# First values loaded plainly and summed on VectorE, second keys and values pooled by TensorE, in a kernel whose order a planner writes

## The chip, the cores and the metric

The kernel runs on one core of a Trainium2 chip. The metric is the device time of one execution in microseconds (us); the median of three runs stands for a kernel. The engines named below are TensorE (PE, its weight loads PEld), VectorE (DVE), ScalarE (ACT), GpSimd (POOL) and SP, which only issues transfers. All transfers share 16 DMA engines.

## The reference, cut to what matters

Three layers follow one another, for 8 sequences of 576 tokens with 8 heads of 64 channels (4608 tokens, 512 channels). Only the first two matter here.

```python
k_p = k.reshape(B, H, 72, 8, D).mean(axis=3)      # pooled keys: 8 tokens to one
v_p = v.reshape(B, H, 72, 8, D).mean(axis=3)      # pooled values
attn = softmax(q @ k_p.T / sqrt(D))               # 576 x 72 for each head
x = attn @ v_p                                    # -> (4608, 512)
h = x @ w_in; g = h * sigmoid(h); y = g @ w_out   # 512 -> 2048 -> 512
```

A third layer routes every token to one of 8 experts or past them.

## The kernel before, in words

**Attention.** The 4608 queries are 36 tiles of 128 tokens. For tile `i` the kernel loads `q` (SP), makes the scores of all heads (`sc_all`, TensorE), the maxima (`mx_all`, VectorE), the exponentials (`ex_half`, ScalarE), their normalisation (`ns_all`, `nr_half`), a transpose (`pt_half`), its copy (`pc_half`), and the product with the pooled values (`pv_all`). `x_copy` (operation `xc`) puts the result into `xs`. A tile needs the pooled keys `kT` and pooled values of the sequences `b` its tokens lie in: tiles 0 to 3 of sequence 0 alone, tile 4 of sequences 0 and 1.

**Pooling.** The first keys (`k_load`, four transfers of 288 KB) arrive plainly and VectorE sums them with a strided reduction (`k_pool`, L325). Everything else is pooled by the DMA engines. For each sequence there are two accumulators for keys (`kA`) and two for values (`vp_at(b)`, `vB`). The first of four slices is loaded plainly by SP, and the other three are added on arrival (`pool_in`, L320, `accum_op=ALU.add`, issued by GpSimd). Each of these 144 KB transfers waits until the one before it on the same accumulator has landed. Then one addition of the two halves follows (`k_half` into `kT`, L333; `v_pool`, L349).

**The dense layer.** Its weights come as 16 transfers of 512 KB (`load_w`, L221, three buffers `stages`). Each is turned into float by two passes of ScalarE (`conv_low` L245, `conv_abs` L241) and two of VectorE (`conv_mix` L249, `conv_or` L254), then split into a high part (ScalarE, L281) and a low part (VectorE, L285). Activations are split likewise (`x_hi` L450, `x_lo` L454). The tokens go in 9 groups of 512; the first two groups use the plain product `whole` (L488, operations `pl`), the later ones a scheme with fewer products (L468). The activated results go through `outs` to memory.

**What sets the order.** `dense()` lists every operation with its possible engines, a cost in us on each, and the operations it waits for. `schedule()` keeps a clock for each engine, for the DMA queue and for buffers, and always takes the ready operation of greatest height: its longest chain of costs to the end, plus a bonus from the table `BONUS` by kind and phase. The order written in this way is fixed; on the chip each engine runs its own list in order, and waits at its head. So SP's transfers, too, wait behind one another. The planner decides on which of two engines some operations run.

```python
op(("k", b, r), {u: cost}, lambda e, b=b, r=r: k_add(b, r), [("k", b, r - 1)] if r % 4 else last_k, ...)
height[n] = min(ops[n][0].values()) + ops[n][4] + max((SIGNAL + height[u] for u in users[n]), default=0)
```

## Time and profile before

| what | us |
|---|---|
| median of 3 runs | 1274.11 |
| lowest and highest | 1271.37, 1277.19 |
| the profiled execution | 1271.41 |
| its span, first to last instruction | 1269.7 |
| TensorE busy in the span | 1219.1 (96%) |
| VectorE busy | 911.3 (72%) |
| ScalarE busy | 635.5 (50%) |
| GpSimd busy | 292.2 (23%) |

TensorE's busy time is an average: the first slices of the span have 30% and 70%, nearly all others 90% or more. The plain DMA queue takes 41.3% of the 16 engines' time for 172.26 MB, the adding and indirect queue 10.7% for 27.72 MB. In the rows further down, L12 is line 12 of the kernel, an arrow in brackets names what ended an engine's idle time, and a tile's buffers have no numbers. TensorE works a float32 product off in two rows, so a product of tile 0's scores (4 calls) shows as x8.

### The profile page before, as it was taken

The numbers are of one execution on the slowest core, as the hardware profiler recorded it, in microseconds if no ns is written. First come the engines' busy times: TensorE is split into PE (matmuls) and PEld (weight loads), VectorE is DVE, ScalarE is ACT, GpSimd is POOL, SyncE is SP. The second block draws the span as 40 slices with busy tenths as digits, with TensorE's granted clock in tenths as the row PEclk, the third lists the DMA queues.
The fourth block names the chain that finished last, engine by engine and source line by source line (L and its number), as shares of the span: only waits on it lengthen the run. The fifth ranks groups of instructions, "written<-read, shape, count | busy, mean of one in ns | idle before, by whom it ended". The sixth has DMA issues, their size and how long they took to land.

```text
span 1269.7 us, 24001 instructions
## 1 busy us (share of the span) xinstructions
PE 1219.1 (96%) x8148; PEld 1092.4 (86%) x8148; DVE 911.3 (72%) x2428; ACT 635.5 (50%) x1802; POOL 292.2 (23%) x289
## 2 busy tenths in 40 slices
PE   3799999999999999999999999999999999999997
PEld 3599989999999999978878888888888888888886
DVE  5786887776777778858988889888973445544572
ACT  5866677778777777722222222323331434443441
POOL 4232122112100000013423324242621212112121
PEclk9899999999999999999999999999999999999999
DMA  8896455646543337764434454454623444455642
GB/s 236 219 224 162 122 125 159 160 149 176 149 144 128 111 126 247 240 252 163 124 127 151 133 163 135 139 159 121 214 100 110 125 164 154 140 168 175 242 154 69
DMA packets 99414, 201.79 MB, mean 159 GB/s; under 512 B 17159, under 2 KB 35591, under 8 KB 99136
## 3 DMA queue, kind: packets, MB, share of 16 engines
q1 hardware_dynamic: 82736, 172.26, 41.3%
q0 software_dynamic: 16528, 27.72, 10.7%
q8 instruction: 71, 1.16, 0.4%
q14 instruction: 79, 0.65, 0.2%
HBM read 173.89 MB, written 66.99 MB: 190 GB/s over the span
## 4 chain that ended last, share of the span: by engine, by line
PE 56%; issue 20%; DMA 9%; DVE 8%; ACT 4%; POOLq 2%; POOL 1%; SPq 0%; another core or an unknown queue 0%; ACTq 0%; DVEq 0%
PE bk L468 17%; PE bk L571 10%; PE bk L572 9%; PE bk L573 9%; PE bk L488 3%; DMA stages<-in_w_in_dram 2%; PE bk L418 2%; PE bk L407 2%; PE bk L377 2%; POOLq L1489 2%; DMA room<-in_v_dram 2%; ACT room L391 1%; DVE room L591 1%; DMA room<-vd 1%; DMA out_dram<-xs,room 1%
## 5 line engine op out<-in xcount | busy, mean ns | idle before, releaser
L468 PE MATMUL bk<-ra,w7h 128*128 128x256 f32 x1088 | 200.6, 284 | 2.1 <-ACT outs L510 1.8
L556 ACT CAST w7h<-outs 128x512 fp32r<-128x512 f32 x142 | 87.8, 622 | 216.2 <-PE bk L572 183.9
L591 DVE SCALAR_TENSOR_TENSOR room<-bk,room 128x512 bf16<-128x512 f32 x272 | 187.9, 691 | 9.0
L571 PE MATMUL bk<-w7h 128*128 128x512 f32 x468 | 184.4, 394 | 1.5 <-ACT w7h L299 1.5
L572 PE MATMUL bk<-w7l,w7h 128*128 128x512 f32 x468 | 182.9, 391 | 0.2 <-DVE w7l L303 0.2
L573 PE MATMUL bk<-w7h,w7l 128*128 128x512 f32 x468 | 182.6, 390 | 0.0
L468 PEld LDWEIGHTS bk<-ra,w7h 128*128 128x128 f32 x1088 | 166.9, 189 | 4.1 <-ACT outs L510 2.8
L468 PE MATMUL bk<-ra,w7l 128*128 128x256 f32 x544 | 152.4, 280 | 0.0
L560 POOL TENSOR_TENSOR w7l<-outs,w7h 128x512 fp32r<-128x512 f32 x70 | 91.0, 1318 | 106.2 <-DVE room L591 80.3
L571 PEld LDWEIGHTS bk<-w7h 128*128 128x128 f32 x468 | 88.2, 188 | 19.7 <-ACT w7h L299 1.9
L1418 PE MATMUL p<-w7h 128*128 128x256 f32 x352 | 100.3, 285 | 4.8 <-PEq L1666 1.7
L573 PEld LDWEIGHTS bk<-w7h,w7l 128*128 128x128 f32 x468 | 88.3, 189 | 18.4
L572 PEld LDWEIGHTS bk<-w7l,w7h 128*128 128x128 f32 x468 | 88.3, 189 | 18.3 <-DVE w7l L303 0.5
L468 PEld LDWEIGHTS bk<-ra,w7l 128*128 128x128 f32 x544 | 102.8, 189 | 0.0
L1421 ACT ACTIVATE w7h<-p 128x256 fp32r<-128x256 f32 x88 | 33.5, 385 | 136.4 <-PE p L1420 123.4
L1419 PE MATMUL p<-w7l,w7h 128*128 128x256 f32 x352 | 99.8, 283 | 0.4 <-DVE w7l L1404 0.2
L1420 PE MATMUL p<-w7h,w7l 128*128 128x256 f32 x352 | 99.6, 283 | 0.0
L1422 DVE SCALAR_TENSOR_TENSOR w7l<-p,w7h 128x256 fp32r<-128x256 f32 x88 | 36.8, 424 | 83.7 <-ACT w7h L1421 60.6
L514 DVE TENSOR_TENSOR outs<-outs,bk 128x256 f32<-128x256 f32 x168 | 69.9, 417 | 35.4 <-PE bk L468 14.0
L488 PE MATMUL bk<-ra,w7h 128*128 128x256 f32 x512 | 93.6, 285 | 1.2 <-DVE ra L454 0.6
L391 ACT ACTIVATE room<-bk,mx 128x72 f32<-128x72 f32 x288 | 89.1, 334 | 9.6 <-PE bk L468 5.6
L468 PE MATMUL bk<-rb,w7h 128*128 128x256 f32 x480 | 91.1, 285 | 2.8 <-ACT outs L510 2.6
(268 smaller groups left out, 2982.1 us busy)
## 6 DMA issues: line engine op xcount, KB each, us to landing
outs<-gd SPq DMA_DIRECT2D x71, 512.0 KB
gd<-outs SPq DMA_DIRECT2D x56, 512.0 KB
outs<-in_w_dram SPq DMA_DIRECT2D x56, 512.0 KB
late<-in_w_dram SPq DMA_DIRECT2D x48, 512.0 KB
room<-in_w_dram SPq DMA_DIRECT2D x44, 512.0 KB
room<-in_q_dram SPq DMA_DIRECT2D x36, 256.0 KB
out_dram<-xs SPq DMA_DIRECT2D x36, 256.0 KB
x2d<-xs SPq DMA_DIRECT2D x36, 256.0 KB
```

Of the source, the lines that this page charges most:

```text
L391: nc.scalar.activation(out=P_t[i][:, h], in_=heads(ps)[:, h % HP], func=ACTF.Exp, scale=esc, bias=mx_t[i][:, h], accum_out=sm_t[i][:, h])
L468: nc.tensor.matmul(out=ps, lhsT=a[:, kk], rhs=b[:, kk], start=first, stop=end, skip_group_check=on)
L488: nc.tensor.matmul(out=ps, lhsT=a[:, kk], rhs=b[:, kk], start=first, stop=end)
L556: nc.scalar.copy(out=hi, in_=src)
L560: eng.tensor_tensor(out=lo, in0=src, in1=hi.bitcast(F32), op=ALU.subtract)
L571: nc.tensor.matmul(out=ps, lhsT=gh[:, ts], rhs=vh, start=first, stop=False)
L572: nc.tensor.matmul(out=ps, lhsT=gh[:, ts], rhs=vl, start=False, stop=False)
L573: nc.tensor.matmul(out=ps, lhsT=gl[:, ts], rhs=vh, start=False, stop=end)
L591: nc.vector.scalar_tensor_tensor(out=junk, in0=x, scalar=scale, in1=wb[:, e * DM:e * DM + DM], op0=ALU.mult, op1=ALU.mult, accum_out=lg_t[ ...
L1418: nc.tensor.matmul(out=ps, lhsT=W1h4[:, kk, m], rhs=xh[:, kk], start=(kk == 0), stop=False)
L1419: nc.tensor.matmul(out=ps, lhsT=W1h4[:, kk, m], rhs=xl[:, kk], start=False, stop=False)
L1420: nc.tensor.matmul(out=ps, lhsT=W1l4[:, kk, m], rhs=xh[:, kk], start=False, stop=(kk == KD - 1))
```

## The change

The first keys stay as they are, but their copy into `kT` becomes an operation of its own (`kc`). The first values get a layout of their own (`v0`, 72 partitions of 8 x 512) and come in two plain transfers (`v_load`, operations `vr 0`, six slices and two slices). VectorE reduces the six in two halves (`v_part`) and adds the other two (`v_rest`, the last is `vc 0`).

The second keys and values come unpooled, tokens on partitions (`kr`, `vr`: each 512 tokens in one transfer and 64 in another). A band matrix of ones, made by GpSimd at the start in the buffer `part`, sums 8 tokens at a time on TensorE: `k_sum` (`kp`, 20 calls of 72 columns) and `v_sum` (`vq`, 5 calls of 512 columns). Copies put the sums where the adding transfers put them before. Sequences 2 to 7 are pooled as before.

The raw tokens lie in buffers that are used later for something else. Hence new waits: the second keys lie in `outs` and `xs`, so the first plain product and `xc` of tile 2 wait for `kp`, the tail of the second keys and `xc` of tile 0 for `vc 0`; the second values lie in a part that later holds the operands of the second group, which wait for `vq`.

The planner charges adding transfers to the queue of all transfers (`ADDS`), which it did not before. Most costs of transfers are smaller (a 512 KB weight load 1.58 instead of 1.95), some others differ slightly, the bonuses have more phases, and all of their values differ.

```diff
@@ -45,34 +45,48 @@
-    "k": {0: 7196.1, 1: -24839.1, 2: -18055.7}, "kput": {0: 9234.7}, "v": {0: 36837.6, 1: -6003.6, 2: -5925},
...
+    "k": {0: 1087.5, 2: -20638.4, 3: -23245.3}, "kput": {0: 11444.8}, "kc": {0: 1225.9, 1: -61.5},
+    "vr": {0: 2969.2, 1: -4389.3}, "vn": {0: -2354.1}, "vc": {0: -5540, 1: 704.2}, "kr": {1: 2437.1},
...
@@ -183,8 +200,15 @@
+        band = part[:, 0:64 + SP]
+            nc.gpsimd.memset(band, 1.0)
+            nc.gpsimd.affine_select(out=band, in_=band, pattern=[[-POOL, 64 + SP]], base=64 * POOL + 1, channel_multiplier=1,
+                                    compare_op=ALU.is_gt, fill=0.0)
+            nc.gpsimd.affine_select(out=band, in_=band, pattern=[[POOL, 64 + SP]], base=POOL - 64 * POOL, channel_multiplier=-1,
+                                    compare_op=ALU.is_gt, fill=0.0)
...
@@ -315,27 +339,71 @@
...
+        def v_load(n):
+            t = (xs[0:SP, 1024:2048] if n else raws[0:SP]).rearrange("p (r c) -> p r c", c=DM)
+            nc.sync.dma_start(out=t, in_=v0[:, 6 * n:6 + 2 * n])
+        def v_part(n):
+            c = slice(n * 256, n * 256 + 256)
+            nc.vector.tensor_reduce(out=vp_at(0)[:, c], in_=raws[0:SP].rearrange("p (r c) -> p c r", c=DM)[:, c], axis=AX.X,
+                                    op=ALU.add)
+        def v_rest(n):
+            a, b, x = xs[0:SP, 1024:1536], xs[0:SP, 1536:2048], vp_at(0)
+            nc.vector.tensor_tensor(out=x if n else a, in0=a, in1=x if n else b, op=ALU.add)
+        raw_t = {"k": (outs[0], xs[:, 1536:2048]), "v": (raws[:, 0:2048], raws[:, 2048:2560])}
+        def raw_load(c, n):
+            src, t = kr if c == "k" else vr, raw_t[c][n]
+            if n:
+                nc.sync.dma_start(out=t[0:64], in_=src[512:576])
+            else:
+                nc.sync.dma_start(out=t.rearrange("p (j c) -> p j c", c=512), in_=src[0:512].rearrange("(j p) c -> p j c", p=128))
+        def raw_at(c, j):
+            t = raw_t[c]
+            return t[0][:, j * 512:j * 512 + 512] if j < 4 else t[1][0:64]
+        def band_at(j):
+            return band[0:128 if j < 4 else 64, 64 - 16 * j:64 - 16 * j + SP]
+        def k_sum(ps):
+            for hp in range(HP):
+                for j in range(5):
+                    nc.tensor.matmul(out=heads(ps)[:, hp], lhsT=raw_at("k", j)[:, hp * 128:hp * 128 + 128],
+                                     rhs=band_at(j), start=j == 0, stop=j == 4)
+        def v_sum(ps):
+            for j in range(5):
+                nc.tensor.matmul(out=ps[0:SP], lhsT=band_at(j), rhs=raw_at("v", j), start=j == 0, stop=j == 4)
+        def k_put(eng, h, ps):
+            p = slice(64 * h, 64 * h + 64)
+            copy(eng, kT[1][p, :, h], heads(ps)[p])
...
@@ -767,40 +841,55 @@
             for hp in range(HP):
-                op(("k", 0, hp), {"S": 1.1}, lambda e, hp=hp: put_in(("k", 0, hp), k_load(hp)))
-                op(("kput", 0, hp), {"V": 0.7}, lambda e, hp=hp: k_pool(hp, st["k", 0, hp]), [("k", 0, hp)])
-            for b in range((tiles * 128 - 1) // S + 1):
-                old = b > 1 and ((b - 1) * S - 1) // 128
-                last_k = [("kh", b - 1, h) for h in range(2)] if b else []
+                op(("k", 0, hp), {"S": 0.89}, lambda e, hp=hp: put_in(("k", 0, hp), k_load(hp)))
+                op(("kput", 0, hp), {"V": 1.13}, lambda e, hp=hp: k_pool(hp, st["k", 0, hp]), [("k", 0, hp)])
+            for h in range(2):
+                op(("kc", 0, h), {"A": 0.33, "V": 0.37}, lambda e, h=h: k_first(e, h), [("kput", 0, hp) for hp in range(HP)])
+            for n in range(2):
+                op(("vr", 0, n), {"S": (2.7, 0.95)[n]}, lambda e, n=n: v_load(n))
+                op(("vn", 0, n), {"V": 1.65}, lambda e, n=n: v_part(n), [("vr", 0, 0)])
+            op(("vn", 0, 2), {"V": 0.6}, lambda e: v_rest(0), [("vr", 0, 1)])
+            op(("vc", 0), {"V": 0.6}, lambda e: v_rest(1), [("vn", 0, n) for n in range(3)])
+            for n, cost in ((0, 3.1), (1, 0.4)):
+                for c in "kv":
+                    op((c + "r", 1, n), {"S": cost}, lambda e, c=c, n=n: raw_load(c, n), [("kput", 0, hp) for hp in range(HP)] if c == "k" else [("vn", 0, 0), ("vn", 0, 1)])
+            ops["kr", 1, 1][2].append(("vc", 0))
+            op(("kp", 1), {"T": 2.7}, lambda e: k_sum(bk["kp", 1]), [("kr", 1, 0), ("kr", 1, 1)], [B(("kp", 1))])
+            op(("vq", 1), {"T": 4.3}, lambda e: v_sum(bk["vq", 1]), [("vr", 1, 0), ("vr", 1, 1)], [B(("vq", 1))])
+            last["kp", 1], last["vq", 1] = keyed(1), [vdone(1)]
+            for h in range(2):
+                op(("kc", 1, h), {"A": 0.3, "V": 0.37}, lambda e, h=h: k_put(e, h, bk["kp", 1]), [("kp", 1)])
+            op(("vc", 1), {"A": 0.48, "V": 0.6}, lambda e: copy(e, vp_at(1), bk["vq", 1][0:SP]), [("vq", 1)])
+            for b in range(2, (tiles * 128 - 1) // S + 1):
+                old = ((b - 1) * S - 1) // 128
+                last_k = keyed(b - 1) + (b == 2) * [("xc", 3)]
                 for r in range(POOL):
-                    u, cost, lag = ("G", 1.1, 3.3) if r % 4 else ("S", 0.55, 0.0)
-                    if b:
-                        op(("k", b, r), {u: cost}, lambda e, b=b, r=r: k_add(b, r), [("k", b, r - 1)] if r % 4 else last_k, linger=(b == 1) * 1.5 + lag if lag else lag)
+                    u, cost, lag = ("G", 1.1, 1.3) if r % 4 else ("S", 0.44, 0.0)
+                    op(("k", b, r), {u: cost}, lambda e, b=b, r=r: k_add(b, r), [("k", b, r - 1)] if r % 4 else last_k, linger=lag)
                     op(("v", b, r), {u: cost}, lambda e, b=b, r=r: v_add(b, r),
-                       [("v", b, r - 1) if r % 4 else b > 0 and ("vput", b - 1), r == 0 and b > 1 and pe("pv", old)], linger=(b == 1) * 1.5 + lag if lag else lag)
+                       [("v", b, r - 1) if r % 4 else vdone(b - 1), r == 0 and pe("pv", old), b == 2 and r == 4 and ("xc", 3)], linger=lag)
                 for h in range(2):
-                    free, cost = [b > 1 and pe("sc", old)], {"V": 0.37, "G": 0.7}
-                    if b == 0:
-                        free, cost = [], {"A": 0.3, "V": 0.37}
-                    done = [("k", b, 3), ("k", b, 7)] if b else [("kput", 0, hp) for hp in range(HP)]
-                    op(("kh", b, h), cost, lambda e, b=b, h=h: k_half(b, h, e), done + free)
+                    op(("kh", b, h), {"V": 0.37, "G": 0.7}, lambda e, b=b, h=h: k_half(b, h, e), [("k", b, 3), ("k", b, 7), pe("sc", old)])
                 op(("vput", b), {"V": 0.6, "G": 1.23}, lambda e, b=b: v_pool(vp_at(b), vp_at(b), vB, e), [("v", b, 3), ("v", b, 7)])
...
-                   [pe("pv", i)] + (s > 0) * [(c, s - 1, k) for c in ("xh", "xl") for k in ((((0, 1), (7, 2)) if s <= PLAIN else ((3, 6), (5, 4)))[th])]
+                   [pe("pv", i), i == 2 and ("kp", 1), i == 0 and ("vc", 0)] + (s > 0) * [(c, s - 1, k) for c in ("xh", "xl") for k in ((((0, 1), (7, 2)) if s <= PLAIN else ((3, 6), (5, 4)))[th])]
+                    if 3 < slot < 7 and not free:
+                        free = [[("vq", 1)]]
-                        deps = [prev, *[("xl", s, k) for k in ((0, 1), (7, 2))[c // 2]], s == 0 and ("wl", p, c % 2)]
+                        deps = [prev or ("kp", 1), *[("xl", s, k) for k in ((0, 1), (7, 2))[c // 2]], s == 0 and ("wl", p, c % 2)]
...
@@ -995,13 +1086,14 @@
-            SHARED = ("ns", "mix", "or", "um", "uo", "wl", "ws", "vl", "xl", "xd", "sv", "nr", "vsum", "vput", "gl", "dot", "kput", "kh", "wc", "ra", "rg",
+            SHARED = ("ns", "mix", "or", "um", "uo", "wl", "ws", "vl", "xl", "xd", "sv", "nr", "vsum", "vput", "vn", "vc0", "gl", "dot", "kput", "kh", "wc", "ra", "rg",
+            ADDS, LAG, PULL = ("k", "v"), 1.0, 0.94
@@ -1076,6 +1168,8 @@
+                        if n[0] in ADDS:
+                            return t, t, max(queue[0], t + c + LAG) + PULL, u
@@ -1097,6 +1191,8 @@
+                if u == "G" and n[0] in ADDS:
+                    queue[0], free[u] = t1, t + ops[n][0][u]
```

## Rows read from the trace of the kernel before

**Rows 1.** Stretches: length, busy us of PE, PEld, DVE, ACT, POOL, PEclk, DMA, GB/s

```profile
0.00:41.40 41.40, 19.42 (x105) 15.14 (x105) 21.91 (x45) 24.45 (x80) 18.00 (x32) 1.00 0.86 220
41.40:85.00 43.60, 36.48 (x323) 34.29 (x323) 36.07 (x77) 36.90 (x120) 13.89 (x16) 0.92 0.89 237
85.00:700.00 615.00, 605.47 (x4667) 562.27 (x4668) 483.02 (x1332) 381.51 (x1267) 105.70 (x107) 1.00 0.53 160
700.00:1269.70 569.70, 557.72 (x3055) 480.75 (x3053) 370.28 (x977) 192.61 (x337) 154.57 (x135) 1.00 0.46 148
```

**Rows 2.** Chain of waits, first 100 us: start us, us, what

```profile
3.58 8.27 DMA room<-in_v_dram
...
12.13 4.61 DMA room<-in_v_dram
...
17.83 6.67 DMA room<-in_v_dram
...
27.15 8.33 DMA stages<-in_w_in_dram
...
39.41 7.92 DMA stages<-in_w_in_dram
...
64.67 6.53 DMA stages<-in_w_in_dram
...
96.39 0.98 PE bk L377 x8
```

**Rows 3.** Timeline of VectorE and ScalarE: start, us, instruction, count, idle before it

```profile
5.00 3.35 DVE L325 TENSOR_REDUCE room<-outs 128x72 f32<-128x576 f32 x3 [5.00 <-DMA outs<-in_k_dram]
...
9.71 0.87 ACT L353 COPY room<-room 64x288 f32<-64x288 f32 x2 [7.08 <-DVE room L325]
...
21.25 0.56 ACT L353 COPY room<-bk 72x512 f32<-72x512 f32 x1
...
24.59 0.69 DVE L349 TENSOR_TENSOR room<-room 72x512 f32<-72x512 f32 x1 [4.85 <-DMA room<-in_v_dram]
...
26.52 0.62 ACT L281 CAST w7h<-cxs 128x512 fp32r<-128x512 f32 x1 [3.49 <-DVE cxs L254]
...
33.64 0.65 ACT L245 ACTIVATE stages<-stages 128x512 int32<-128x512 uint32 x1 [1.43 <-DMA stages<-in_w_in_dram]
...
47.35 0.67 ACT L245 ACTIVATE stages<-stages 128x512 int32<-128x512 uint32 x1 [2.60 <-DMA stages<-in_w_in_dram]
```

**Rows 4.** Timeline of TensorE

```profile
10.68 2.26 PE L377 MATMUL bk<-room 128*128 128x144 f32 x8 [10.68 <-ACT room L353]
...
25.42 1.97 PE L418 MATMUL bk<-room 72*64 72x128 f32 x16 [1.84 <-DVE room L349]
...
41.43 0.39 PE L488 MATMUL bk<-ra,w7h 128*128 128x256 f32 x1 [0.61 <-DVE ra L454]
...
57.60 1.90 PE L407 MATMUL bk<-ident,room 128*72 128x128 f32 x8 [4.85 <-ACT ra L450]
```

**Rows 5.** DMA queues, 10.5 to 16 us: packets, MB, share of 16 engines

```profile
q1 hardware_dynamic: 677, 1.43, 69.8%
```

**Rows 6.** DMA queues, 35 to 41 us

```profile
q0 software_dynamic: 425, 0.53, 56.9%
```

**Rows 7.** DMA issues of the whole run: count, KB each, median us to landing

```profile
room<-in_v_dram POOLq DMA_DIRECT2D x48, 144.0 KB, 3.5
room<-in_k_dram POOLq DMA_DIRECT2D x42, 144.0 KB, 4.4
```

**Rows 8.** Groups, 0 to 85 us: count, busy us, mean ns, idle before

```profile
L249 DVE SCALAR_TENSOR_TENSOR cxs<-cxs,stages 128x512 int32<-128x512 int32 x16 | 10.8, 688 | 7.1 <-ACT cxs L241 7.0
...
L245 ACT ACTIVATE stages<-stages 128x512 int32<-128x512 uint32 x16 | 10.8, 675 | 9.1 <-DMA stages<-in_w_in_dram 8.9
...
L281 ACT CAST w7h<-cxs 128x512 fp32r<-128x512 f32 x16 | 9.7, 628 | 4.3 <-DVE cxs L254 4.3
```

**Rows 9.** Stretch of 10 us, columns as in rows 1

```profile
15.00:25.00 10.00, 6.47 (x24) 5.17 (x24) 3.81 (x10) 6.47 (x25) 3.52 (x4) 1.00 0.93 206
```

More of the change, by code (lines that the diff above doesn't have):

```diff
@@ L331, in k_half @@
             a, c = (t[ps].rearrange("p (a b) -> p a b", b=SP) for t in kA)
-            if b:
-                eng.tensor_tensor(out=out, in0=a, in1=c, op=ALU.add)
-            else:
-                copy(eng, out, a)
+            eng.tensor_tensor(out=out, in0=a, in1=c, op=ALU.add)
         def k_add(b, r):
-            pool_in(kA[r // 4], k[b - 1, r], r % 4)
+            pool_in(kA[r // 4], k[b - 2, r], r % 4)
         def vp_at(b):
@@ L445, in x_op @@
                 second()
-            t = rings[n // 7]
-            return [t[:, n % 7 * 1024 + a * 512:n % 7 * 1024 + a * 512 + 512] for a in range(2)]
+            if 3 < n < 7 and len(rings[0]) < 2:
+                raw_x.close()
+                ring_b = first_x.enter_context(tc.tile_pool(name="ring_b", bufs=1, side="right"))
+                rings[0].append(ring_b.tile([128, 3 * 1024], F32R, name="rc"))
+            t, n = (rings[1], n - 7) if n > 6 else (rings[0][n // 4], n % 4)
+            return [t[:, n * 1024 + a * 512:n * 1024 + a * 512 + 512] for a in range(2)]
         def x_hi(s, k):
@@ L802, in valued @@
                 def valued(i):
-                    return [("vput", b) for _, _, b in runs(i * 128, 128)]
+                    return [vdone(b) for _, _, b in runs(i * 128, 128)]
                 if i <= JOIN:
@@ L1038, in schedule @@
             known, wide = {}, {"V": [], "G": []}
-            queue, ran, quiet, kind = [3.9], [0.0], [-9.0], [False]
+            queue, ran, quiet, kind = [3.2], [0.0], [-9.0], [False]
             def earliest(n):
```

92 lines of the change are left out of this document (53 added, 39 removed), and 59 rows, old and new, of the table BONUS.

## The prediction

> **What bounds the kernel now.** I read the table of stretches first. TensorE is idle for 21.98 us (41.40 less 19.42) before the first product of the dense layer, for 7.12 us from there to 85 us, for 9.53 us from 85 to 700 us and for 11.98 us in the rest [rows 1]. From 85 us on it is 98% busy, so a change of the loading can pay in the first 85 us alone, and whatever it adds to TensorE after that is paid in full.
>
> The chain of waits of the first 100 us says what that start waits for. Up to 24.5 us it is one series of transfers of the first values: an adding transfer may start only when the one before it has landed, and the steps take 8.27, 4.61 and 6.67 us [rows 2]. After that the chain names loads of `w_in` four times, three of which are shown, with 8.33, 7.92 and 6.53 us from issue to landing [rows 2]. The timeline shows what stands still meanwhile: VectorE idles 4.85 us before it adds the two halves of the values (L349), ScalarE idles 3.49 us behind that for a weight part, and 1.43 and 2.60 us for weight loads [rows 3]. TensorE's first value product of tile 0 comes at 25.42 us, its first product of the layer runs on from 41.43 us, and at 57.60 us it has waited 4.85 us once more [rows 4].
>
> The DMA view says why these loads take so long. From 10.5 to 16 us the plain queue moves 1.43 MB in 69.8% of 5.5 us: 2.68 us of all 16 engines for a MB. From 35 to 41 us the adding queue moves 0.53 MB in 56.9% of 6 us: 6.44 us for a MB [rows 5, 6]. An adding transfer occupies the engines 2.4 times as long, and nothing else gets that time.
>
> **The change, part by part.** *Adding transfers.* 6 of the first values and 12 of the second keys and values go, of 90 in the run (48 + 42) [rows 7]. Each has 144 KB, so 18 x 0.147 = 2.65 MB become plain: 2.65 x (6.44 - 2.68) = 10.0 us of engine time less, nearly all of it before 45 us. The bytes stay the same.
>
> *The first values.* VectorE now sums them: two reductions of 1536 elements a partition, strided as in the four reductions of the keys (L325: 3.35 us for 3 of 576 elements, 1.12 each [rows 3]), so 2.98 us each; and two additions of 512 like L349, 0.69 each. That is 7.3 us in place of 0.69. The lower bound of a reduction goes by the nearest unstrided row, 688 ns for 512 elements (L249 [rows 8]): 2.06 us. I take 2.98, since that row is a strided reduction too. The cover is VectorE's idle time: it is busy for 3.81 of the 10 us from 15 to 25 [rows 9]; if the planner puts the sums in front of tile 0's softmax instead, tile 0 pays for what does not fit. The page "VectorE: DVE Perf Modes" of the Trainium skill (section "Mode 1× (REGULAR) — the baseline", its clock under "Specifications") gives one element a cycle at 0.96 GHz. By it a reduction would take an estimated 1.6 us and the start would come up to 2.8 us earlier still; this trace disagrees, with 1.94 ns an element in L325.
>
> *The front.* Tile 0's value product then waits for its own softmax, whose last copy (L353) ends at 21.81 us [rows 3], so it can start at about 21.9 instead of 25.4: 3.5 us. Tile 1 and the weights behind it shift along. Faster loads take the 1.43 us wait at 33.64 us and about 2 us of the queueing behind it. I take 7 us, first product at 34.4. The bounds are 0 (another wait takes the place, rival 2) and 10: ScalarE is busy 24.45 us before 41.4 [rows 1], at most 2.6 of them before the 7.08 us of idle time that end at 9.71 [rows 3], so the same work ends no earlier than about 31.6. The page "DMA: Bandwidth & Descriptors" of the Trainium skill (section "Why a DMA increments its semaphore by 16 and not by 1") speaks against part of this: a transfer of 72 partitions gets 12 of the 16 engines, the largest divisor up to 16. By that rule the plain load of the values would take an estimated third longer, about 1 us, and the sum would be 1 us smaller; no row shown here counts a transfer's engines.
>
> *41 to 85 us.* Lost here are the 7.12 us of idle time and, by the granted clock of 0.92 [rows 1], about 2.9 us of half-rate work after the gap before 57.60 us. Faster landings should close a part only, since ScalarE (36.90 of 43.60 us) and VectorE (36.07) are over 80% busy. If ScalarE became unbroken, 6.7 us could come back; I take 4. The lower end is a loss of 2, if the bulk loads stand before the weights.
>
> *TensorE's new sums.* A score product of tile 0 has 4 calls of 144 columns: 0.98 us late, 2.26 us at the start [rows 2, 4], that is 1.70 ns a column late. The granted clock reads 1.00 for the front [rows 1], yet the same calls take 2.3 times as long there, as at the lower level of 1.2 GHz. `v_sum` has 5 x 512 = 2560 columns: 4.35 us. `k_sum` has 20 x 72 = 1440: 2.45 us, 5.6 us at the early rate, and up to 4.9 us if not the columns but its 40 short rows set the pace (0.98 us for 8). The first product of the layer now waits for `k_sum`, so this one lies in TensorE's idle front: nothing. `v_sum` is needed only before the second group's operands and falls into the full stretch: 4.35 us in full (bounds: 0 if it too finds a hole, 10.0 at the early rate; the nearest row is that of a full stretch).
>
> *Moved and added waits.* The second keys' tail waits for `("vc", 0)`, and SP issues in order, so every later load, weights first, queues behind that wait. The bulk loads are 2.36 MB, 6.3 us of all engines; but the same bytes stood ahead of 42 us already, so I take nothing, and 6.3 us as the upper end (rival 2). Three short GpSimd instructions for the band are covered, as `kT` is first written at 9.71 us [rows 3]. ScalarE's `xc` of tiles 0 and 2 wait for sums that are due before them. The new costs and bonuses reorder the rest of the run: 9.53 us of idle time lies there up to 700 us [rows 1], and I take nothing, with 3 us to either side.
>
> Sum: -7 - 4 + 4.35 = -6.65 us on the profiled execution of 1271.41 us: 1264.8. That execution is at the fast end of three (1271.37 to 1277.19); the median is 2.7 us above it. I put the new median about 1.2 above its sum: 1266 us.
>
> **Rivals.** *1. Given back* (about 1273 us). By 85 us all 16 weight loads are converted: 2 x 0.675 (two passes of one kind) + 0.628 = 1.98 us of ScalarE for each, 31.6 us, and three passes of VectorE at 0.69 each about 33 us [rows 8], beside seven tiles of attention. If these conversions are the limit, products start earlier and then wait for weights: the 85 us point moves by 3 to 4 us only and `v_sum` takes it back: 1271.4 - 3.5 + 4.35, and 1.2 as above. For it: both engines over 80% busy from 41 to 85. Against it: their idle time before weights is named DMA.
>
> *2. The gate* (about 1281 us, slower). The first product waits for `k_sum`, that for the tail of the second keys, that for `("vc", 0)` on VectorE, which has 7.3 us of sums in front of it, with all of SP's later loads behind. If `k_sum` ends after about 39 us, the front gains nothing; 4.35 and 2.45 us of sums and some 2 us of later weights are added: 1271.4 + 8.8 + 1.2. For it: SP already stood long behind waits, and the DMA engines were 86% busy in the front [rows 1]. Against it: VectorE has 6.19 us of idle time from 15 to 25 us [rows 9], so the wait should be over by about 22 us.
>
> *3. Everything fits* (about 1257 us). The third weight load and tile 2 come after the first product, which moves 13 us, and all 6.7 us come back: -13 - 6.7 + 4.35 = -15.4, and 1.2. For it: an earlier start also leaves less time at half rate. Against it: all three engines would have to be nearly full at once.
>
> **How the numbers follow.** Forecast 0.46 (own range 1261 to 1270), given back 0.22, the gate 0.20 (1278 to 1288), everything fits 0.12. A change within 0.5% (6.4 us) can't be told from none here, so faster means below 1267.7 us: the third rival and three quarters of the forecast, 0.46. Slower means above 1280.5 us: seven tenths of the gate and a little of rival 1, 0.16. The rest, 0.38, is no change. The range 1254 to 1282 takes in the unknown 3 us of the rest of the run and leaves out the better third of rival 3, the worse half of the gate and the tails.
>
> **What would show it.** Right: tile 0's value product near 22 us and the first product of the layer near 34; `k_sum` ended before 30; under 6 us lost from there to 85; `v_sum` as 4.3 us in a full stretch; TensorE idle time before 85 us of about 18 instead of 29 us. Wrong: reductions of the values near 1.6 us; a first product that waits for `k_sum`; ScalarE waiting for loads of `w_in` as long as before; or more than 3 us of difference after 85 us, where I see none.

## The result and the profile after

The changed kernel takes 1290.26 us (median of 6 runs, 1279.97 to 1294.09) against 1272.48 of the kernel before beside it (6 runs): a ratio of 1.0123, 95% interval 1.0088 to 1.0159. It is slower, and the forecast of 1266 us, faster, was wrong in sign. The profiled execution took 1291.52 us with a span of 1289.5, 19.8 more than the span before.

The stretches of the changed kernel (columns as in [rows 1]):

```profile
0.00:41.40 41.40, 20.01 (x87) 16.62 (x87) 24.85 (x39) 19.78 (x70) 4.81 (x19) 1.00 0.76 235
41.40:85.00 43.60, 38.96 (x297) 31.53 (x297) 28.11 (x58) 33.67 (x101) 9.54 (x10) 0.92 0.56 158
85.00:700.00 615.00, 605.37 (x4714) 564.76 (x4713) 485.61 (x1296) 385.93 (x1290) 121.14 (x120) 1.00 0.54 160
700.00:1289.50 589.50, 572.84 (x3104) 492.76 (x3103) 392.95 (x1023) 196.35 (x345) 155.08 (x139) 0.99 0.45 147
```

TensorE is hardly less idle in the front than before (21.39 us against 21.98), and from 41.4 to 85 us the DMA engines fell from 89% to 56% and VectorE from 36.07 to 28.11 us: the work that should have come sooner comes later. TensorE's timeline says where (start, us, instruction, calls, idle before):

```profile
28.04 1.12 PE L486 MATMUL bk<-room 72*64 72x128 f32 x8 [0.56 <-ACT room L421]
...
33.82 1.82 PE L382 MATMUL bk<-part,outs 128*128 128x72 f32 x8
...
43.19 0.70 PE L382 MATMUL bk<-part,xs 64*128 64x72 f32 x2
...
45.72 6.53 PE L387 MATMUL bk<-raw,part 128*72 128x512 f32 x10
...
53.97 0.49 PE L560 MATMUL bk<-ra,w7h 128*128 128x256 f32 x2
```

Tile 0's value product (L486) comes at 26 to 29 us, against 25.42 [rows 4]; `k_sum` (L382) takes 10.1 us, `v_sum` (L387) 6.53, and the first plain product (L560) follows at 53.97 instead of 40.4. VectorE and ScalarE in the same time:

```profile
13.30 5.45 DVE L356 TENSOR_REDUCE room<-raw 72x256 f32<-72x1536 f32 x2 [4.62 <-DMA raw<-in_v_dram]
18.67 0.80 DVE L451 TENSOR_REDUCE mx<-bk 128x4 f32<-128x288 f32 x2
```

```profile
15.94 0.66 ACT L269 ACTIVATE stages<-stages 128x512 int32<-128x512 uint32 x1 [6.36 <-DMA stages<-in_w_in_dram]
...
43.93 0.80 ACT L421 COPY room<-bk 64x288 f32<-64x288 f32 x2 [5.78 <-PE bk L382]
...
47.88 0.68 ACT L269 ACTIVATE stages<-stages 128x512 int32<-128x512 uint32 x1
```

The value reductions (L356) stand ahead of tile 0's maxima (L451), whose scores were done at 11.94. At 43.93 ScalarE has waited 5.78 us for `k_sum`, and the next weight pass (L269) stands behind that copy in its list, at 47.88: the conversions of `w_in` stop while TensorE sums keys.

For each kernel the table has, from one profiled execution, the start of the first and last plain product, the end of the 16th weight conversion (`conv_or`, VectorE), the first product of the second layer and that layer's length (first to last start), and the timed ratio to before with its interval (none for undo_second, whose time can't be compared). Its rows are explained under the experiments.

| kernel | first product | 16th conversion | last plain product | second layer from | its length | ratio |
|---|---|---|---|---|---|---|
| before | 40.4 | 84.8 | 172.1 | 530.5 | 400.4 | |
| after | 54.0 | 96.9 | 185.5 | 547.7 | 406.8 | 1.0123 [1.0088, 1.0159] |
| again | 46.0 | 89.0 | 177.6 | 538.8 | 410.2 | 1.0193 [1.0120, 1.0266] |
| swap | 49.3 | 94.8 | 183.4 | 544.1 | 408.9 | 1.0177 [1.0132, 1.0223] |
| tail_before | 46.5 | 90.5 | 179.1 | 540.2 | 397.4 | 1.0068 [1.0042, 1.0094] |
| before_tail | 39.4 | 83.2 | 170.5 | 529.1 | 412.1 | 1.0121 [1.0084, 1.0157] |
| undo_second | 43.9 | 89.4 | 178.0 | 544.8 | 404.0 | |
| tile0_first | 43.6 | 86.9 | 175.5 | 538.2 | 406.9 | 1.0162 [1.0099, 1.0226] |
| vector_lo | 47.9 | 91.4 | 180.0 | 542.4 | 409.6 | 1.0083 [1.0053, 1.0113] |
| v0_before | 40.2 | 84.7 | 172.0 | 530.5 | 400.2 | 0.9998 [0.9973, 1.0023] |
| k1_before | 55.1 | 99.5 | 188.6 | 545.7 | 394.4 | 1.0085 [1.0057, 1.0113] |
| both_before | 45.7 | 86.0 | 173.2 | 530.6 | 398.5 | 0.9996 [0.9973, 1.0019] |
| weights_both | 44.7 | 83.7 | 171.0 | 529.5 | 394.8 | 1.0008 [0.9986, 1.0030] |
| weights_after | 52.1 | 94.1 | 182.7 | 546.5 | 410.6 | 1.0109 [1.0081, 1.0137] |
| tail_last | 46.4 | 90.7 | 180.0 | 541.8 | 397.6 | 1.0100 [1.0063, 1.0137] |
| weights_more | 47.7 | 86.8 | 174.1 | 532.3 | 395.8 | 0.9989 [0.9968, 1.0011] |
| weights_pool | 47.7 | 86.5 | 173.7 | 532.6 | 394.7 | 1.0037 [1.0010, 1.0063] |

So the 19.8 us of the two profiles are: first product +13.6, plain products -0.2 (131.7 and 131.5), later products of the first layer +3.8 (358.4 and 362.2), second layer +6.4, third layer -3.8 (338.8 and 335.0 from there to the end of the span).

Near the end of the second layer TensorE waits for GpSimd. GpSimd's timeline, then TensorE's:

```profile
934.67 1.00 POOL L727 DMA_INDIRECT lst<-row,du  x1 [4.55 <-DMA lst<-row,du]
935.69 1.30 POOL L632 TENSOR_TENSOR w7l<-outs,w7h 128x512 fp32r<-128x512 f32 x1
937.15 1.04 POOL L1468 DMA_INDIRECT late<-x2d,room  x1 [0.16 <-issue]
938.50 1.01 POOL L1468 DMA_INDIRECT late<-x2d,room  x1 [0.31 <-issue]
939.54 2.48 POOL L632 TENSOR_TENSOR w7l<-outs,w7h 128x512 fp32r<-128x512 f32 x2
```

```profile
942.08 0.79 PE L645 MATMUL bk<-w7h,w7l 128*128 128x512 f32 x1 [4.32 <-POOL w7l L632]
942.67 0.63 PE L643 MATMUL bk<-w7h 128*128 128x512 f32 x1
```

Low parts of the last chunk (L632) stand behind a list write that waits 4.55 us for a transfer and behind two gathers for the experts (L1468). TensorE loses 4.32 us, and the products behind that take 0.63 us instead of 0.39. None of this touches the pooling: it comes with the order drawn anew.

### The profile page after: what moved, and what is told of

Same layout as the page of the kernel before. It is cut to its first block, busy times and chain, and to the rows that moved or that the text cites. A ratio compares the mean times of both kernels' runs of the same rounds, so it can differ in the third digit from the quotient of the medians.

```text
span 1289.5 us, 24104 instructions
## 1 busy us (share of the span) xinstructions
PE 1237.2 (96%) x8198; PEld 1105.7 (86%) x8198; DVE 931.5 (72%) x2414; ACT 635.7 (49%) x1805; POOL 290.6 (23%) x288
## 5 line engine op out<-in xcount | busy, mean ns | idle before, releaser
L644 PE MATMUL bk<-w7l,w7h 128*128 128x512 f32 x468 | 183.4, 392 | 0.0
L540 PE MATMUL bk<-ra,w7h 128*128 128x256 f32 x608 | 113.8, 283 | 0.9 <-ACT outs L582 0.8
L632 POOL TENSOR_TENSOR w7l<-outs,w7h 128x512 fp32r<-128x512 f32 x70 | 90.1, 1310 | 97.8 <-ACT w7h L628 97.5
L644 PEld LDWEIGHTS bk<-w7l,w7h 128*128 128x128 f32 x468 | 88.6, 189 | 18.0
L643 PEld LDWEIGHTS bk<-w7h 128*128 128x128 f32 x468 | 88.6, 189 | 17.9
L540 PEld LDWEIGHTS bk<-ra,w7h 128*128 128x128 f32 x608 | 93.3, 189 | 1.5 <-ACT outs L582 1.2
L540 PE MATMUL bk<-rc,w7h 128*128 128x256 f32 x480 | 90.8, 283 | 3.2 <-ACT outs L582 2.2
L727 POOL DMA_INDIRECT lst<-row,du x36 | 39.1, 1087 | 232.2 <-DVE du L724 159.6
L592 ACT ACTIVATE t<-outs 128x256 f32<-128x256 f32 x168 | 70.3, 427 | 36.4 <-DVE outs L586 28.8
```

Of the source, the lines that this page charges most:

```text
L540: nc.tensor.matmul(out=ps, lhsT=a[:, kk], rhs=b[:, kk], start=first, stop=end, skip_group_check=on)
L592: nc.scalar.activation(out=t, in_=ps[:, 0:CH] if m == 3 else part_of(n, SUM[m]), func=ACTF.Tanh, scale=0.5)
L632: eng.tensor_tensor(out=lo, in0=src, in1=hi.bitcast(F32), op=ALU.subtract)
L643: nc.tensor.matmul(out=ps, lhsT=gh[:, ts], rhs=vh, start=first, stop=False)
L644: nc.tensor.matmul(out=ps, lhsT=gh[:, ts], rhs=vl, start=False, stop=False)
```

## The experiments

Theories after the comparison: the *front* (TensorE's sums, in its list ahead of the first product, hold the layer back), the *new order* (the planner's redrawn list costs time far from the edit), and *loads* (the bulk loads of the raw tokens hold up `w_in`, as my rival 2 had it).

**again**: the changed kernel, unedited, to see how its profile repeats.

> The changed kernel once more, unaltered, as the measure for the others. Front theory (the pooled sums on TensorE, 10.1 and 6.5 us in its list ahead of the first product, are the loss): first product of the layer at 54 us again, last product of that layer near 547.5, 17 us later than before; about 1288 us. Rival (the loss lies in the re-drawn order after the front, with the 4.3 us wait for GpSimd near 938 us): that wait of over 4 us returns in this profile. If it does not, it belongs to single executions and not to the plan.

The median is the same, 1290.26 (1285.09 to 1301.49); the ratio is 1.0193 instead of 1.0123, because the kernel before took 1269.95 us beside it and 1272.48 in the first comparison. Ratios of two comparisons can differ by that much. But in its profile `k_sum` runs at TensorE's upper rate almost throughout (eight rows in about 1.1 us, where the first profile has 1.98), and ScalarE waits 1.35 us for it instead of 5.78:

```profile
33.08 1.01 PE L382 MATMUL bk<-part,outs 128*128 128x72 f32 x8
...
38.25 0.44 PE L382 MATMUL bk<-part,xs 64*128 64x72 f32 x2
...
39.64 4.66 PE L387 MATMUL bk<-raw,part 128*72 128x512 f32 x10
...
46.02 0.49 PE L560 MATMUL bk<-ra,w7h 128*128 128x256 f32 x2
```

```profile
38.72 0.80 ACT L421 COPY room<-bk 64x288 f32<-64x288 f32 x2 [1.35 <-PE bk L382]
```

5.6 us for `k_sum`, 4.66 for `v_sum`, first product at 46.0. So 8 of the 13.6 us of the front belong to one execution, some 7 of them to its rate; the second layer is 410.2 us all the same, and the wait for L632 is there again (4.1 us). Front figures are compared with this profile from here on.

**short_both** and **short_loads**: both sum one block of the second tokens in five; short_loads also leaves out four fifths of the loads. Tokens of that sequence then go to other experts, so only what lies ahead of the third layer can be compared.

```diff
-                for j in range(5):
+                for j in range(1):
...
-            if n:
-                nc.sync.dma_start(out=t[0:64], in_=src[512:576])
...
+            if n == 0:
+                nc.sync.dma_start(out=t[:, 0:512], in_=src[0:128])
```

> Leaves out four of the five token blocks of both pooled sums of the second sequence (8 rows instead of 40 for its keys, 2 instead of 10 for its values); order, loads and waits stay. Front theory: the key sum takes about 2.0 us instead of 10.1 and the value sum about 1.7 instead of 6.5, so the first product comes at about 41 instead of 54 us and the whole run is about 13 us shorter, near 1275. Rival loads (the bulk loads of 2.36 MB and SP's waits hold the weights back): first product and time stay within 3 us of the changed kernel. Rival order: the same, within 3 us.

> As the kernel with both sums shortened, and of the second keys and values only the first 128 tokens are loaded (0.5 MB instead of 2.36 MB, the tails not at all). Front theory: the loads are hidden, so within 2 us of the kernel with the shortened sums alone (about 1275 us, first product near 41 us). Rival loads: the weights behind them come 5 to 6 us earlier, the first product too, and the time falls by as much again, to about 1269.

The first plain product comes at 41.1 and 41.4 us, the first layer's end at 541.3 and 540.5. The bulk loads cost nothing that can be seen (under 1 us either way): *loads* falls. Without most of the sums the first product is 4.9 us sooner than in again, yet the 16th conversion comes only 2.0 us sooner (87.0), the plain products end 1.5 us sooner, and the first layer ends no sooner (538.8 there): the first product is not what sets that end. The 13 us that the front theory expected can't be read from the times, 1325.77 and 1324.14 us: with other tokens for the experts the third layer is some 37 us longer than in again.

**swap**: `v_sum` ahead of `k_sum`.

```diff
+            at = [n for n, _ in program]
+            program.insert(at.index(("kp", 1)), program.pop(at.index(("vq", 1))))
```

> The value sum (5 calls of 512 columns) is put right ahead of the key sum (20 calls of 72 columns) in TensorE's list; nothing else moves. If TensorE's rate in the front is the matter, the clock comes up during the wide calls, as it did in the changed kernel, and the key sum then takes about 5 us instead of 10.1: first product at about 49 us instead of 54, and about 5 us less in all (1283). If the key sum is slow by itself, whatever the clock, it takes 10 us again and the time stays within 2 us of the changed kernel.

No gain: 1291.35 us. `k_sum` took 5.7 us and the first product came at 49.3, as expected; but again has 5.6 us without the swap, and beside it the first product is 3.3 us and the 16th conversion 5.8 us later. So the front is no better for the swap, and the time does not show that it is worse.

**tail_before** and **before_tail**: each kernel with the other's list (engines and banks included) from the last product of the first layer on; **tail_last**: the changed kernel with the list of before for the last 219 operations alone, the last three chunks of the second layer and what follows.

```diff
+            cut = max(i for i, (n, _) in enumerate(program) if n[0] == "mm") + 1
+            program[cut:] = tail
```

> The changed kernel, but from the last product of the first layer on every instruction stands in the order that the kernel before has there (with its engines and banks); all ahead of it is as changed. Theory (a part of the loss is the second half's new order, drawn afresh by the planner): the second layer lasts about 401 us as before instead of 407 to 410, the wait of TensorE for GpSimd's w7l of 4.1 to 4.3 us is gone, and the time is 1281 to 1284 us, 6 to 10 less than the changed kernel's. Rival (the second layer is longer for another reason, such as what the first layer leaves behind): second layer 407 to 410, time 1290.

> The kernel before, but from the last product of the first layer on every instruction stands in the changed kernel's order. Theory of the new order: second layer 407 to 410 us, the wait for w7l of about 4 us appears, time 1276 to 1280, 6 to 10 more than before. Rival: no more than 2 us from the kernel before.

The order decides, and it goes with the list both ways. In each line: calls of one product of the second layer, its shortest, middle and longest duration in ns, first and last start.

```profile
L730 PE MATMUL bk<-w7h x468: 389/389/628, 540.2 to 937.6; 128*128 128x512 f32 x156
```

```profile
L658 PE MATMUL bk<-w7h x468: 389/389/628, 529.1 to 941.2; 128*128 128x512 f32 x156
```

The changed kernel with the old tail has a second layer of 397.4 us, and its ratio falls to 1.0068; the kernel before with the new tail has 412.1 us and rises to 1.0121, with not one instruction of the change in it. That is as much as the whole change in the first comparison (1.0123) and two thirds of it in the second (1.0193). The profile of before_tail is of the fastest of its six executions and has only 7.1 us of the 16.6 between the medians (11.7 more in the second layer, 3.2 less in the third, 1.4 less ahead); where the others lose more no profile shows.

> The changed kernel through the end of the second layer's fifteenth chunk; the last 219 operations (the last three chunks and what runs beside them) stand in the order of before. Theory (the loss sits in the last chunks, where GpSimd's gathers and list writes stand ahead of low parts): no wait for w7l, second layer 399 to 403 us, time 1280 to 1284. Rival (it is spread): second layer 405 or more, time 1286 or more.

```profile
L925 PE MATMUL bk<-w7h x468: 389/389/498, 541.8 to 939.4; 128*128 128x512 f32 x156
```

397.6 us, with no wait for a low part: in this profile the last three chunks are all of it. The time, 1280.62 us, is that of tail_before within the intervals. All profiles narrow it down to the last chunk: from the first to the last of its 26 calls of one line it takes 17.2 us in every kernel with the old order there, and 23.8 to 26.6 us in every kernel with the new one, always with a wait for a low part of 3.8 to 6.9 us. The time up to it overlaps: 377.2 to 383.3 us in the old order, 379.4 to 386.9 in the new. The busy time of one of the three product lines in the stretch from 350 to 400 us after the layer's first product shows the loss too, before first, then after (length, busy us and calls, granted clock, DMA share, GB/s):

```profile
880.00:930.00 50.00, 28.57 (x73) 1.00 0.57 188
```

```profile
897.70:947.70 50.00, 25.12 (x62) 0.93 0.56 190
```

**vector_lo**: one edit at that place, the last chunk's low parts all on VectorE.

```diff
+            program = [(n, "V" if n[0] == "gl" and n[1] == 17 else u) for n, u in program]
```

> The changed kernel with one edit: the second layer's last eight low parts (gl of chunk 17) all run on VectorE; five of them stood on GpSimd behind its gathers and list writes. Theory (that place in the new order costs most of the second layer's 6 to 10 us: the wait of about 4 and the half rate behind it): no wait of TensorE for GpSimd's w7l, second layer 400 to 403 us, time 1282 to 1285. Rival (the wait moves to VectorE, whose list is as full there): a wait for DVE's w7l of 3 us or more, second layer still 406 or more, time 1289 to 1291.

```profile
PE bk L645 <- DVE w7l L632: 6.9, 1, 6.9
```

(Waits of TensorE: us, times, longest.) The wait moved to VectorE and grew to 6.9 us, as the rival had it; the second layer is 409.6 us. The median, 1282.5, lies in the range of the theory, though the profiled execution, 1288.93, is the longest of its four. The experiment leaves open whether the engine matters; the order of the three chunks as a whole does.

**undo_second**: the changed kernel with the second keys and values pooled by adding transfers again, put into the changed order by hand. The third values' first transfer overwrites half of the second values ahead of their sum, so here too only the first two layers compare, and the time, 1288.79 us, does not.

```diff
+            gone = [("kr", 1, 0), ("kr", 1, 1), ("vr", 1, 0), ("vr", 1, 1), ("kp", 1), ("vq", 1), ("kc", 1, 0), ("kc", 1, 1), ("vc", 1)]
...
+            program = [x for x in program if x[0] not in gone]
+            put_after(("kc", 0, 1), (("k", 1, 0), "S"), (("k", 1, 4), "S"))
...
+            put_after(("xl", 0, 1), (("kh", 1, 0), "V"), (("kh", 1, 1), "V"))
```

> The changed kernel with the second sequence's keys and values pooled by adding transfers again (12 on GpSimd's queue, two DVE halves and one sum), TensorE's 50 calls gone; the rest keeps the changed order. Theory (TensorE's sums in its in-order list hold the first product back by their own length, the first values bring nothing): first plain product at 41 to 44 us instead of 46 to 54, time 1278 to 1284. Rival 1 (the adding transfers take the engines that w_in needs, as my prediction had it): first product near 41 but the plain products 4 us longer than 131.8. Rival 2 (the late tile 0 sets the front whoever pools the second keys): first product still at 46 or later.

First product at 43.9 us, the 16th conversion at 89.4 (89.0 in again), last plain product at 178.0 (177.6). TensorE's 50 calls gone, the plain products end where they did. I had looked at the wrong mark, the first product, and so had the three theories. The end of the plain products follows another mark in all 19 profiles (the table's and the two short ones): it comes 87.2 to 89.3 us behind the 16th conversion of `w_in`, while the first product lies between 39.4 and 55.1 us. That is a regularity; which of the two holds the other it does not show.

**tile0_first**: tile 0's softmax ahead of the value sums (VectorE) and of the first weight pass (ScalarE); its transposes ahead of tile 1's scores. A part of the list, operations as in the kernel's text:

```diff
-sc:0 vn:0:0 vn:0:1 low:0:0 abs:0:0 mx:0 vr:1:0 vr:1:1 low:0:1 vn:0:2 ex:0:0 mix:0:0 vc:0 low:0:2 or:0:0 q:2 ex:0:1 sc:1
+sc:0 mx:0 ex:0:0 vn:0:0 ex:0:1 ns:0 nr:0:0 nr:0:1 low:0:0 abs:0:0 pt:0:0 mix:0:0 pt:0:1 sc:1 or:0:0 pc:0:0 low:0:1 q:2
+w:0:3 wh:0:0 vn:0:1 vr:1:0 vr:1:1 pc:0:1 vn:0:2 vc:0 kr:1:1
```

> The changed kernel with tile 0's softmax taken ahead of the value sums on VectorE (the first of the two reductions runs beside the exponentials, the second behind the division) and ahead of the first weight pass on ScalarE; second q's scores behind tile 0's transposes. Theory (the sums in front of tile 0's softmax cost the front what the freed queue gained): pt of tile 0 at 18 to 20 us instead of 23.9, k_sum starts at 29 to 31 instead of 33.8, first product 3 to 5 us earlier than in the changed kernel at the same TensorE rate, time 1285 to 1288. Rival (second keys and their DMA set k_sum, or weights set the first product): k_sum not before 33 or first product within 1 us of the changed kernel's.

```profile
16.73 1.89 PE L480 MATMUL bk<-ident,room 128*72 128x128 f32 x8 [5.34 <-DVE room L475]
...
22.75 1.20 PE L491 MATMUL bk<-room 72*64 72x128 f32 x16 [2.04 <-DVE room L366]
```

Transposes at 16.73 instead of 23.94, value product at 22.75, `k_sum` at 30.65, first product 2.4 us and 16th conversion 2.1 us sooner than in again. The time (1286.62) does not show it beyond its interval. The caveat of my prediction on the place of the sums was real and worth about 2 us.

**v0_before**, **k1_before**, **both_before**: the first half of the change, the second, and both, all with the order of before for everything else. both_before has the front of tile0_first up to the first plain product, so the changed kernel's own front was not run in the old order. The lists are written out:

```diff
+            program = [name(x) for x in LIST_ORDER.split()]
+            for x in LIST_BANK.split():
+                n, b = name(x)
+                bk[n] = banks[int(b)]
```

> The first half of the change alone, in the order of the kernel before: first values by two plain loads, two VectorE reductions (one behind tile 0's division, one behind tile 1's maxima) and two sums; the second sequence by adding transfers; all else in the order of before. Theory (the values' own work on VectorE, 2.73 us each, takes the place of the 4.85 us wait that goes): first product 39 to 42 us against 40.4, second layer 400, time within 4 us of before. Rival (my prediction: the freed transfers bring the front forward): first product 34 to 36, time 1262 to 1266.

> The second half alone, in the order of the kernel before: second keys and values loaded plainly and pooled by TensorE's 50 calls (keys behind tile 1's transposes, values behind its pv, as the change has them); first values by adding transfers as before. Theory (TensorE's list holds the front back by the length of these calls): first product 5.5 to 13 us later than before, at 46 to 53, later stages as before, time 1275 to 1283. Rival (idle time of TensorE in the front hides them): first product by 43, time within 3 us of before.

> The whole change, with the front in the order of the kernel tile0_first up to the first plain product, and everything behind that in the order (engines and banks) of the kernel before. Theory (what the change itself costs is the front, 3 to 6 us; the rest of the loss is the new order): first product 43 to 46, first layer ends at 533 to 537, second layer 398 to 402, time 1272 to 1277. Rival (the later stages are longer because of what the change leaves behind): first layer's rest or second layer longer than before by 4 us or more, time 1280 or more.

The whole change, with the mended front and the old order behind it, is 0.9996 of before: it costs nothing and brings nothing. The first half alone: 0.9998. Its TensorE timeline answers to [rows 4]:

```profile
25.05 1.98 PE L769 MATMUL bk<-room 72*64 72x128 f32 x16 [0.47 <-DVE room L644]
...
40.19 0.56 PE L843 MATMUL bk<-ra,w7h 128*128 128x256 f32 x2
```

The 4.85 us wait for the adding transfers [rows 3] is gone and VectorE's sums stand in its place; tile 0's value product moves by 0.4 us, the first product by 0.2. The second half alone costs 0.85%: in the old front `k_sum` starts at 34.04 and the conversions pause from 39.7 to 57.9 us, while ScalarE waits 8.3 and 5.5 us for products that stand behind the sums in TensorE's list. That 0.85 and 0 give 0 together is no sum: both_before also has tile 0 and with it `k_sum` 3.7 us sooner, and in k1_before's profile `k_sum` ran at the lower rate; how the 0.85% divides between the two is not settled. In both_before the first product is 5.3 us later than before and the 16th conversion only 1.2, and the plain products end 1.1 us later. VectorE's conversion rows, before, after and both_before (start, us, count; the 16th is the last):

```profile
83.52 1.28 DVE L254 SCALAR_TENSOR_TENSOR cxs<-stages,cxs 128x512 int32<-128x512 int32 x2
```

```profile
96.20 0.68 DVE L278 SCALAR_TENSOR_TENSOR cxs<-stages,cxs 128x512 int32<-128x512 int32 x1
```

```profile
84.68 1.29 DVE L560 SCALAR_TENSOR_TENSOR cxs<-stages,cxs 128x512 int32<-128x512 int32 x2
```

**weights_both** and **weights_after**: both_before and tile0_first with the passes over weights 4 to 6 and the next loads ahead of the copies that wait for TensorE. **weights_more**: further passes moved likewise. **weights_pool**: also the first values' sums on GpSimd. The list of the first of them, and the sums of the last:

```diff
-low:0:4 or:0:3 ex:2:0 w:0:6 low:0:5 pv:1 q:4 ex:2:1 vq:1 kc:1:0 ns:2 kc:1:1 nr:2:0 xc:1
-nr:2:1 wh:1:1 xh:0:0 wl:1:1 xh:0:1 xl:0:0 low:0:6 xl:0:1 abs:0:4 abs:0:5 mix:0:4
+or:0:3 low:0:4 abs:0:4 mix:0:4 ex:2:0 w:0:6 low:0:5 abs:0:5 or:0:4 w:0:7 mix:0:5 or:0:5 w:0:8 q:4 pv:1 ex:2:1
+wh:1:1 low:0:6 abs:0:6 vq:1 kc:1:0 ns:2 kc:1:1 nr:2:0 xc:1 nr:2:1 wl:1:1 mix:0:6 or:0:6 w:0:9 xh:0:0 xh:0:1
...
+                    nc.gpsimd.tensor_tensor(out=acc, in0=rows[0] if i == 1 else acc, in1=r, op=ALU.add)
```

> As both_before, but the passes over weights 4 to 6 (ScalarE and VectorE) and the loads of weights 7 to 9 stand ahead of tile 1's copies and of the two copies of the pooled keys, which wait for TensorE. TensorE's list is that of both_before. Theory (the sixteenth weight conversion sets the plain products' end, about 88 us behind it): the gap in the conversions from 31.7 to 42.6 us is filled, the sixteenth comes at 78 to 84 us instead of 86.0, the plain products end by 167 to 171 instead of 173.4, time 1262 to 1267, with the first product still at 44 to 47. Rival (TensorE's list sets it): plain products end within 1 us of 173.4 though the conversions come earlier, time 1268 to 1271.

> As tile0_first (the changed kernel, tile 0's softmax first), with the same weights' passes and loads moved ahead; all behind keeps the changed order. Theory: sixteenth conversion at 80 to 85 us instead of 86.9, plain products end at 168 to 174 instead of 175.6, time 1279 to 1284. Rival: plain products end at 175 to 177, time 1285 to 1288.

> As weights_both, with the passes over weights 7 and 8 and the loads of weights 10 and 11 moved ahead too (behind tile 0's and 1's first splits and behind tile 2's scores' maxima instead of behind the first tanh and tile 4's). Theory (the sixteenth conversion sets the plain products' end): sixteenth at 77 to 82 us instead of 83.7, plain end at 165 to 169.5 instead of 171.1, time 1262 to 1267. Rival (cx buffers, loads or TensorE's idle lists take over): sixteenth at 83 or later, or plain end at 170.5 or later although it comes sooner; time 1267 to 1271.

> As weights_more, with the first values' eight rows summed by seven additions on GpSimd instead of two reductions and two additions on VectorE (6.9 us of VectorE's list), and the first low part on VectorE. Theory (VectorE's front is full, GpSimd's empty): first conversions 3 to 6 us sooner than in weights_more, sixteenth 2 to 4 us sooner, time 1258 to 1265. Rival (GpSimd's additions end later than 24 us and hold tile 0's pv, or share what VectorE reads through): pv of tile 0 at 24 or later, sixteenth conversion not sooner, time 1266 or more.

weights_both: 16th conversion 2.3 us sooner than both_before, end of the plain products 2.2 sooner, with TensorE's list unchanged: the end went with the conversions, though the first product, too, came 1.0 us sooner. But the theory's size failed: the pause moved from 31.7 to 42.6 us to 39.0 to 51.2, and the time is that of before. In weights_after `k_sum` ran at the lower rate and ended at 42.0; the 16th conversion came at 94.1, not 80 to 85, the plain products' end 88.6 behind it. Its median, 1283.6, lies in the range of the theory all the same, so the time does not bear the theory out. weights_more moved the pause again (47.7 to 66.0) and the 16th came 3.1 us later than in weights_both: its rival, with the plain end 87.3 behind. On GpSimd the seven additions take 10.2 us from first to last:

```profile
12.37 1.26 POOL L644 TENSOR_TENSOR room<-raw 72x512 f32<-72x512 f32 x1 [9.16 <-DMA raw<-in_v_dram]
13.70 5.48 POOL L644 TENSOR_TENSOR room<-room,raw 72x512 f32<-72x512 f32 x4
19.27 3.27 POOL L644 TENSOR_TENSOR room<-room,xs 72x512 f32<-72x512 f32 x2
```

Taking them off VectorE changed the 16th conversion by 0.3 us, and the time is 0.37% above before, which its front does not explain. No version here beats the kernel before.

## Why the prediction was wrong

**The step that cost most: "The new costs and bonuses reorder the rest of the run ... and I take nothing, with 3 us to either side."** The reordered rest is 6.4 us net in the two profiles (+3.8, +6.4, -3.8), and exchanging the tail alone moves the time by 1.2% (before_tail). Every kernel with the new order of the second layer has it at 404.0 to 412.1 us, every one with the old order of its last part at 394.4 to 400.4; the first layer's part between plain products and second layer is 357.1 to 358.9 us in the old order and 360.7 to 366.8 in the new. The diff showed that nearly every bonus had changed. With the old tail the changed kernel keeps 0.68% (tail_before); with the old order of the rest of the first layer and the mended front as well, nothing (both_before). I sized the term by the 9.53 us of idle time there, as if an order could only move idle time about; it can also add waits where there were none, with work at the lower rate behind them. No rival carried it.

**"I take 7 us, first product at 34.4": failed.** It came at 54.0 and 46.0, against 40.4 before (41.4, from which I counted, is the layer's second call). Three parts of the step fell. (a) The place of the sums, my own caveat: tile 0's maxima waited for both reductions; put in front (tile0_first) its value product comes at 22.75, near the 22 I named. (b) "The first product of the layer now waits for `k_sum`, so this one lies in TensorE's idle front: nothing." It lies at 33.8 to 43.9 or 33.1 to 38.7, between tile 1's transposes and its value product, and at the lower rate the weight passes queued behind the copies on ScalarE pay for it: 5.78 us of waiting in the first profile, and a 16th conversion at 96.9 us instead of 89.0. At the upper rate the wait is 1.35 us, and four fifths of the sums are worth 2.0 us of that conversion (short_both); so the rest of its lag behind 84.8 us lies in the front's order, of which tile0_first mends 2.1. I asked what the instruction hides behind, not what stands behind its consumers. (c) The freed transfers: 18 adding transfers did go (36 and 36 are left of [rows 7]), and v0_before shows them worth 0.2 us of the first product, since VectorE's sums fill the gap.

**"41 to 85: I take 4": not in the changed kernel** (the plain products take 131.5 against 131.7 us). In both_before they take 127.5, and this pays for the later first product. Faster landings do not explain it by themselves, as v0_before has 131.8. The conversions fit: they went on during the front, so that six weights were ready or nearly so at the first product (45.7 us), against five before (40.4 us). No run separates this from the rest of the front.

**Sizes.** Reductions: 2.98 us predicted, 2.73 measured in the change's row; the 1.6 us that I worked out from the Trainium skill's page "VectorE: DVE Perf Modes" (section "Mode 1× (REGULAR) — the baseline") did not come. `v_sum`: 4.35 predicted, 4.66 at the upper rate (again), 6.53 in the first profile. `k_sum`: 2.45, 5.6 or 4.9 named, 5.6 and 10.1 measured; the 40 short rows do set the pace, 0.14 us each at the upper rate and 0.25 at the lower: the case of 4.9 and the early rate apply together. That the 5.6 named for the early rate is what the upper rate gave is chance.

**The rivals.** *Given back* had the mechanism (the conversions as the limit) and the wrong sign, since I let the change only speed them up. *The gate* had the sign, at 1281, and its condition came true in the first profile (`k_sum` ended at 43.9, behind 39); but not by the chain that I gave, SP's loads behind `vc 0`: short_loads takes the loads away and the first layer ends within 1 us. Its 8.8 us are about what stays without the new tail (0.68%, 8.6 us), by luck, since the chain was another; the new order of the second layer, which no rival had, is the rest of the loss (17.8 and 20.3 us between the medians of the two comparisons). The range's upper end, 1282, left out a case in which front and order both lose.

**The signs that I had named.** Of the wrong ones three came: a first product behind `k_sum`, ScalarE waiting for `w_in` nearly as long (6.4 us in the first 60, 7.3 before), and more than 3 us after 85 (6.4 net, as above). Of the right ones none came in the changed kernel; TensorE's idle time before 85 us is 26.0 us (21.39 and 4.64 by the stretches), not 18, though 16.6 us of sums were added to its work.

## What to carry to other kernels

Where a planner draws the order, an edit changes two things, and the second may be larger: run the old kernel with the new order of a part that the edit doesn't touch (here the second layer) before explaining anything by the edit. With in-order lists, ask of a new instruction not only what it hides behind, but what stands behind those who wait for it. Take as the mark of a start not its first product but one that its end keeps step with: here a count of converted weights, 88 us ahead.

## What the runs showed of the hardware that was not expected

The same list of TensorE reaches its upper rate at different times. In again and in the changed kernel's profile the score product of tile 2 is alike (2.13 us from 30.63, 2.12 from 31.05); then the next transposes take 0.69 in the one and 1.06 in the other, and `k_sum` runs at the upper rate from 33 us in the one and at the lower to its end at 43.9 in the other. The granted clock reads 1.00 for this stretch in both. What decides it no run showed.

`k_sum`'s calls of 72 columns cost 0.14 us a row at the upper rate (5.6 us for 40), where `v_sum`'s of 512 columns cost 0.47 (4.66 for 10): 7.1 times the columns for 3.3 times the time. On GpSimd an addition of 72 x 512 took 1.26 to 1.59 us against 0.69 on VectorE.
